# A 64-column product behind the first unit's products, and two planner costs, in an fp32 recurrence with a bilinear feed-forward block

## Chip, cores and metric

The kernel runs on one core of one Trainium2 chip. The metric is device microseconds of one launch. TensorE (PE, with its weight loads PEld), VectorE (DVE), ScalarE (ACT), GpSimd (POOL) and SyncE (SP, which issues most of the DMAs) each work through a queue of their own, in order.

## What is computed

A gated linear recurrence over 4 batches x 8 heads, 768 steps, head size 48, and behind it a bilinear feed-forward block on the 3072 rows of 384 channels that it gives:

```python
f = 1.0 / (1.0 + np.exp(-f_logit))
for t in range(S):
    state = f[:, :, t, :, None] * state + np.einsum('bhd,bhe->bhde', k[:, :, t], v[:, :, t])
    y[:, :, t] = np.einsum('bhd,bhde->bhe', q[:, :, t], state)
...
x = y.transpose(0, 2, 1, 3).reshape(B * S, H * D)
out = ((x @ w_a) * (x @ w_b)) @ w_out     # 384 -> 1536 -> 384
```

## The kernel before

**Attention.** The recurrence is cut into 16 units of four heads and half a sequence (384 steps), and a unit into six chunks of 64 steps. The front of a unit (`front_parts`) forms two sigmoids on ACT (L323, L326), an affine step on POOL (L329), running products by scans on DVE (L333, L346), and multiplies them into k and q (L350). Then follow on TensorE `scores` (L396), `turn` (L421, copied by `turned` on ACT, L428 and L430), `gains` (L445), `within` (L504) and `across` (L530), all with small tiles; on DVE `mask` (L409) and `carry` (L472, L474), which adds the chunks' gains up to states, six or five sums per unit. `across` adds what the states before a chunk give to the chunk. `out_of_bank` (L553) copies the result out of PSUM, and DMAs (L575) store it to `xT`, transposed as the feed-forward block wants it.

**Feed-forward.** Rows go through in eight blocks of 384. The first two blocks use `up` (L619): per 128 features six products of 384 columns, ACT's copy of one factor (L640) and DVE's product (L645), while the float64 weights are still being loaded and converted (`from_double`, L71 to L83). Later blocks use `up_triples` (L745): 15 block products v1 to v5, v6, u1 to u5, r2, r3, t1, t2 in place of 18, for each of four triples j. ACT copies results out of PSUM (L1333, the line where the planner calls a step), DVE adds them (L737). At the end of a triple, `finish` issues v6, its copy, and the product a * b over 1152 columns, also in L737. `finish` of triple j runs inside triple j+1. Copies of the next triple reuse buffers that the sums and the product read. `down` (L847) multiplies by `w_out` with seven products for eight, copied and added on ACT and DVE (L862 to L882).

**Order.** For the first 19 of the 24 feature groups of the two first blocks the order is written by hand. There `across(0)` of the first unit follows `gains(1)`, then come its copies and stores (`y_of(0)`), further carried sums of unit 1, `across(1)`, and two unread products of 384 columns (`keep_up`) that only keep TensorE going:

```python
across(0)
y_of(0)
end(1)
carried(1, range(1, NJ - 1))
first_scan, *scans = parts[2][1]
emit_all([first_scan])
across(1)
keep_up(2, ps_y[:, 0])
```

The rest is ordered by a list planner when the program is built. `main` is the list of feed-forward steps in fixed order, where every TensorE step counts as a beat of 653 ns. Attention steps lie in six lines (`core`, `fore`, `loads` and so on), each with an engine, an assumed cost in ns and an offset. Before each main step, `fill` takes steps from the lines that fit. A step for another engine fits only if `delays` says no: `delays` walks the next 80 main steps and asks whether main steps of this engine, each with a load and a due beat, would end after the start of the TensorE beat that they are due for. A due of 0 means that a step has no due beat. The assumed costs are 870 for a scan L333, 385 for a scan L346, 880 for a product L350 or a mask, 930 and 750 for the sigmoids, 400 for a copy in a triple, 180 for a `carry`, 1280 for a triple's product.

Of the kernel before, what the change touches and what calls it, by code (L numbers as in the profile page):

```python
# [18 lines left out]
ALU = mybir.AluOpType  # L19
# [3 lines left out]
BLK = 384  # L23
# [7 lines left out]
SUB = 64  # L31
# [122 lines left out]
def by_quotients(ctx, tc, q, k, f_logit, v, moe_w_a, moe_w_b, moe_w_out, out, ident, weights, bad, ps_f):  # L154
    nc = tc.nc
# [21 lines left out]
    def fixed(shape, name):  # L177
        return fixedp.tile(shape, FP32, tag=name, name=name)
# [3 lines left out]
    for i in range(NSET):  # L182
        t = {n: fixed([128, 2, BLK], f"{n}_in{i}") for n in "qkf"}
# [28 lines left out]
    def unit(u):  # L212
        b, r = divmod(u, NH * NQ)
        return (b, *divmod(r, NQ))
# [89 lines left out]
    PE, DVE, ACT, POOL, SP = range(5)  # L304
    live = {}
    firsts = groups[:, len(EARLY)].rearrange("p (u n s) -> p u n s", u=NQ, n=2)
    products_of_f = {u: firsts[:, u] if u in FIRST else sets[u % NSET]["f"] for u in range(NU)}
    xT = {}

    def halves(x):  # L310
        return x.rearrange("p n s -> p (n s)")
# [48 lines left out]
    ps_x, ps_y = (ps_a.tile([128, 2, 512], FP32, tag=n, name=n) for n in ("ps_x", "ps_y"))  # L360
    idle = list(range(4))

    def tokens(n, c, p):

        return slice(n * BLK + c * C + p * SUB, n * BLK + c * C + p * SUB + SUB)

    def each():
        for n in range(2):
            for c in range(NC):
                yield n, c, (n * NC + c) * SUB  # L370
# [142 lines left out]
    def across(u):  # L513

        b, half, qd = unit(u)
        qf, st, ps = halves(sets[u % NSET]["q"]), live[u]["st"], live[u]["y"]

        order = [(n, c, o, p) for n, c, o in each() for p in range(2)]
        if u in FIRST:

            order = sorted(order[::-1], key=lambda x: -x[3])
        elif half:
            order = [(n, c, o, p) for n, c, o in reversed(list(each())) for p in range(2)]
        for n, c, o, p in order:
            j = 2 * c + p
            if j == half == 0:
                continue
            for h in range(2):
                r, e = slice(R * h, R * h + D), R * (p ^ h)
                nc.tensor.matmul(  # L530
                    ps[p][e:e + D, o:o + SUB],
                    lhsT=st[j][r, n],
                    rhs=qf[r, tokens(n, c, p)],
                    start=False,
                    stop=True,
                    skip_group_check=True,
                )
# [49 lines left out]
    def products(blk):  # L587

        first = (NTG, 0)[blk] if blk < 2 else blk % 2
        return groups[:, first:first + NTG].rearrange("p g (k t) -> p g k t", k=NFT)  # L590
# [11 lines left out]
    def on(engine, load, due, do, *args, copied=False):  # L602
        return engine + COPIED * copied, load, beats[0] + due if due else 1 << 30, do, *args
# [46 lines left out]
    NI, NJ3 = 3, NFT // 3  # L650
# [88 lines left out]
    def up_triples(blk):  # L739

        to, tail = products(blk), None

        def emit(ps, name, j, start):
            for g in range(2):
                nc.tensor.matmul(  # L745
                    ps[:, g],
                    lhsT=sums_of_w[name][:, g, 128 * j:128 * j + 128],
                    rhs=sums_of_x[blk][name],
                    start=start and g == 0,
                    stop=True,  # L750
                    skip_group_check=True,
                )

        def times(ps, name, j, start=False):
            return on_pe(BEAT, emit, ps, name, j, start)

        def copy(due, x, ps):
            return on(ACT, 400, due, nc.scalar.copy, x, ps)

        def finish(j, c, out, v):  # L760
            yield times(v, "v6", j)
            yield copy(5, out[1, 0], v)
            a, b = (
                c[:, g].rearrange("p k i t -> p k (i t)").rearrange("p k (g t) -> p g k t", g=NTG) for g in range(2)
            )
            yield on(DVE, 1280, 0, add_steps, to.rearrange("p g (k j) t -> p j g k t", k=NI)[:, j], a, b, ALU.mult, copied=True)

        for j in range(NJ3):
            v, u, r, t = (ps_f[i][:, 0:BLK].rearrange("p (g t) -> p g t", g=2) for i in free)
            free[:] = [free[i] for i in ((2, 1, 3, 0) if j < NJ3 - 1 else (2, 3, 1, 0))]  # L770
            c = (sums, last[:, 0:2 * NI * BLK])[j % 2].rearrange("p (g k i t) -> p g k i t", g=2, k=NI, i=2)
            out = {(k, i): c[:, :, k, i] for k in range(NI) for i in range(2)}
            if j % 2:
                at = thirds.index(down_first[0])
                pairs = [thirds[(at + n) % 3] for n in (1, 2)]
            else:
                pairs = [last[:, PIECE * n:PIECE * n + PIECE] for n in range(2)]
            first, second = (x.rearrange("p (g n t) -> p g n t", g=2, n=2) for x in pairs)

            def add(due, k, i, ps, copied=False):  # L780
                return on(DVE, 550, due, add_steps, out[k, i], ps, out[k, i], copied=copied)

            yield times(v, "v1", j, True)
            yield copy(3, out[2, 0], v)
            if tail:
                yield from finish(*tail)
            yield times(u, "u1", j, True)
            yield copy(3, out[1, 1], u)
            yield times(r, "r2", j, True)
            yield add(6, 1, 1, r, True)  # L790
            yield times(v, "v2", j)
            yield copy(3, out[2, 1], v)
            yield times(u, "u2", j)
            yield copy(3, first[:, :, 1], u)
            yield times(t, "t1", j, True)
            yield copy(6, out[0, 0], t)
            yield times(v, "v3", j)
            yield copy(3, first[:, :, 0], v)
            yield on(DVE, 870, 0, add_steps, c[:, :, 1:3, 1], c[:, :, 1:3, 1], first, copied=True)
            yield times(u, "u3", j)  # L800
            yield copy(3, out[0, 1], u)
            yield times(r, "r3", j, True)
            yield add(6, 2, 1, r)
            yield times(v, "v4", j)
            yield copy(3, second[:, :, 1], v)
            yield times(u, "u4", j)
            yield add(3, 0, 0, u)
            yield times(t, "t2", j)
            yield add(5, 0, 1, t)
            yield times(v, "v5", j)  # L810
            yield copy(2 if j == NJ3 - 1 else 3, second[:, :, 0], v)
            yield times(u, "u5", j)
            yield add(3, 2, 0, u)
            yield on(DVE, 870, 0, add_steps, c[:, :, 0], c[:, :, 0], second, copied=True)
            tail = j, c, out, v
        yield from finish(*tail)

    down_first = [thirds[0]]

# [106 lines left out]
    def core_parts(s):  # L926


        u = s - 1
        if u < 2 * NQ:  # L930
            yield PE, 1000, 0, scores, s
        elif s < NU:
            yield PE, 1600, 0, within_and_scores, u
        else:
            yield PE, 1000, 20 * BEAT, within, u
        if s < NU:
            yield DVE, 880, 0, mask, s
            yield PE, 760, 0, turn, s
            yield ACT, 700, 0, turned, s
        if u < 2 * NQ:  # L940
            yield PE, 1000, 0, gains, s
        elif s < NU:
            yield PE, 1550, 0, gains_and_across, u
        else:
            yield PE, 1000, 0, across, u
        if s < NU:
            for j in range(NJ - 1 if unit(s)[1] == NH - 1 else NJ):
                yield DVE, 180, 0, carry, s, j
            if unit(s)[1] < NH - 1:
                yield DVE, 320, 0, hand_on, s  # L950
        if u >= 2 * NQ:
            for part in range(3):
                yield ACT, 490, 0, out_of_bank, u, part
            begin, *stores = stores_of(u)
            yield SP, 0, 0, begin
            for do in stores:
                yield SP, ISSUE, 5000, do
# [41 lines left out]
    with tc.manual_schedule():  # L999
# [12 lines left out]
            for _, _, do, *args in steps:  # L1012
                do(*args)

        def keep_up(n, to):

            x = products_of_f[0][:, 0]
            for _ in range(n):
                nc.tensor.matmul(to[:, 0:BLK], lhsT=ident, rhs=x, start=True, stop=True)

        def y_of(u):
            for part in range(4 if u == NQ - 1 else 3):
                out_of_bank(u, part)
            stored(u)
            if u == NQ - 1:
                give_back(live[u]["y"])
# [40 lines left out]
        within(1)  # L1067
        gains(1, range(NC - 1, NC))
        across(0)
        y_of(0)  # L1070
        end(1)
        carried(1, range(1, NJ - 1))
# [98 lines left out]
        for blk in range(NBLK):  # L1171
# [5 lines left out]
            b, odd = divmod(blk, 2)  # L1177
# [508 lines left out]
```

## Time and profile before

| | |
|---|---|
| Runs | 594.01, 592.02, 594.11 us; median 594.01 |
| Profiled execution | 591.24 us, its span 589.2 us |
| Busy PE, DVE, ACT, POOL | 567.3, 410.6, 258.1, 88.5 us |
| PE rows | L619: 288 rows of 384 columns, mean 490 ns; L745 and L847: rows of 192 columns, mean 326 to 331 ns |
| Prologue, 0 to 34 us | PE busy 18.5 us |
| 34 to 126 us; 126 to 186 us | PE busy 92.0; 59.9 us |
| 186 to 235; 235 to 300; 300 to 390 us | PE busy 47.9 of 49; 64.9 of 65; 89.9 of 90 us |
| 390 to 589 us | PE busy 194.3 of 199 us |

The page gives busy time, the chain that ended last, and groups of instructions by line. An fp32 product appears on PE as two rows, and as two weight loads on PEld. A row's length is modelled and overlaps the next row's; the distance of two starts tells the pace. In the timeline a line is a run of like rows: start, length, engine, line, tiles, count, and in brackets the idle time before it with what ended it. "issue" means that the engine waited for nothing that the profile shows.

### The profile page before, as it was taken

Reading aid. Unit: us, or ns where it says so; the run is one execution under the profiler, and the core shown is the slowest. Engines: PE = TensorE matmul, PEld = TensorE weight load, DVE = VectorE, ACT = ScalarE, POOL = GpSimd, SP = SyncE. Lnnn points to the kernel's source line nnn. Section 1 sums busy time; section 2 is a strip of 40 time slices with the busy share of each in tenths; the row PEclk is TensorE's granted clock in tenths of the full one; section 3 lists DMA queues with packets and bytes.
Section 4 is the critical chain, followed back from the end, with each engine's and each line's share of the span. In section 5 each row is a group of like instructions: output and inputs, shape, how many; then the busy total and the mean of one; then the engine's idle time right before and its main releaser. Section 6 shows DMA issues by size and latency. Waiting matters only on the chain.

```text
span 589.2 us, 13937 instructions
## 1 busy us (share of the span) xinstructions
PE 567.3 (96%) x5794; PEld 510.0 (87%) x5794; DVE 410.6 (70%) x782; ACT 258.1 (44%) x494; POOL 88.5 (15%) x73
## 2 busy tenths in 40 slices
PE   2889999999999999999999999999999999999996
PEld 1656655558999999999999999999999999999996
DVE  6898544699878768877896687928784256745741
ACT  5588768642133553247521355335431345144300
POOL 6465557462000000000000000000000000000000
PEclk9999999999999999999999999999999999999999
DMA  8699399099442403044004400040001100000001
GB/s 208 190 265 312 110 291 252 0 184 189 124 120 63 101 2 102 10 122 101 2 12 118 129 1 2 5 125 21 3 1 48 48 1 0 2 28 1 0 29 32
DMA packets 33576, 49.42 MB, mean 84 GB/s; under 512 B 3984, under 2 KB 25280, under 8 KB 33504
## 3 DMA queue, kind: packets, MB, share of 16 engines
q1 hardware_dynamic: 30000, 42.19, 25.9%
q0 software_dynamic: 3088, 5.92, 5.9%
q8 instruction: 47, 0.77, 0.6%
q10 hardware_dynamic: 416, 0.34, 0.2%
q14 instruction: 25, 0.20, 0.1%
HBM read 33.23 MB, written 4.72 MB: 64 GB/s over the span
## 4 chain that ended last, share of the span: by engine, by line
PE 90%; DVE 5%; issue 2%; DMA 1%; ACT 1%; SPq 0%; DVEq 0%; ACTq 0%
PE ps_f L745 37%; PE ps_f L847 28%; PE ps_f L619 16%; PE ps_y L504 2%; PE ps_x L396 2%; PE ps_x L445 1%; PE ps_y L530 1%; PE ps_x L421 1%; DVE sums L737 1%; DVE inv L346 1%; DVE groups L333 1%; DMA f_in<-in_f_logit_dram 1%; DVE q_in L350 1%; DMA xT<-groups 0%; DVE groups L737 0%
## 5 line engine op out<-in xcount | busy, mean ns | idle before, releaser
L619 PE MATMUL ps_f<-xT,w_ba 128*128 128x384 f32 x288 | 95.7, 490 | 2.8 <-DMA xT<-y 2.6
L619 PEld LDWEIGHTS ps_f<-xT,w_ba 128*128 128x128 f32 x288 | 53.7, 190 | 39.8 <-DVE start L341 3.2
L1333 ACT COPY sums<-ps_f 128x384 f32<-128x384 f32 x120 | 57.6, 481 | 69.6 <-PE ps_f L745 61.4
L1333 ACT COPY groups<-ps_f 128x384 f32<-128x384 f32 x120 | 57.8, 481 | 59.4 <-PE ps_f L745 39.0
L745 PE MATMUL ps_f<-xT,w_ba 128*128 128x192 f32 x384 | 78.5, 327 | 0.0
L745 PEld LDWEIGHTS ps_f<-xT,w_ba 128*128 128x128 f32 x384 | 64.8, 190 | 0.2
L73 POOL TENSOR_SCALAR sums<-sums 128x768 f32<-128x768 f32 (+1 forms) x20 | 51.2, 2561 | 33.6 <-ACT sums L71 33.5
L745 PE MATMUL ps_f<-groups,w_ba 128*128 128x192 f32 x288 | 55.1, 327 | 0.0
L745 PE MATMUL ps_f<-x_sums,raw 128*128 128x192 f32 x288 | 54.2, 331 | 0.7 <-DVE sums L737 0.6
L329 POOL TENSOR_SCALAR inv<-inv 128x768 f32<-128x768 f32 x14 | 12.7, 904 | 261.6 <-ACT inv L326 237.6
L847 PE MATMUL ps_f<-w_out,groups 128*128 128x192 f32 x288 | 51.8, 329 | 0.0
L847 PE MATMUL ps_f<-w_out,sums 128*128 128x192 f32 x288 | 51.4, 326 | 0.0
L745 PEld LDWEIGHTS ps_f<-x_sums,raw 128*128 128x128 f32 x288 | 46.9, 190 | 3.5 <-DVE sums L737 1.1
L847 PE MATMUL ps_f<-spare,sums 128*128 128x192 f32 x288 | 49.6, 327 | 0.0
L745 PEld LDWEIGHTS ps_f<-groups,w_ba 128*128 128x128 f32 x288 | 48.0, 190 | 0.2 <-ACT groups L1333 0.2
L847 PEld LDWEIGHTS ps_f<-w_out,groups 128*128 128x128 f32 x288 | 47.2, 190 | 0.7
L847 PEld LDWEIGHTS ps_f<-w_out,sums 128*128 128x128 f32 x288 | 47.4, 190 | 0.1
L847 PEld LDWEIGHTS ps_f<-spare,sums 128*128 128x128 f32 x288 | 47.0, 190 | 0.2
L737 DVE TENSOR_TENSOR sums<-ps_f,sums 128x384 f32<-128x384 f32 x60 | 32.8, 553 | 15.5 <-PE ps_f L745 14.2
L737 DVE TENSOR_TENSOR sums<-sums,groups 128x768 f32<-128x768 f32 x36 | 34.7, 963 | 12.4 <-ACT groups L1333 12.0
L745 PE MATMUL ps_f<-xT,raw 128*128 128x192 f32 x192 | 39.6, 329 | 0.5 <-ACT sums L1333 0.5
L745 PE MATMUL ps_f<-x_sums,w_ba 128*128 128x192 f32 x192 | 39.3, 327 | 0.1
(150 smaller groups left out, 848.0 us busy)
## 6 DMA issues: line engine op xcount, KB each, us to landing
raw<-w_ba POOLq DMA_DIRECT2D x11, 512.0 KB, 8.3
k_in<-in_k_dram SPq DMA_DIRECT2D x32, 144.0 KB, 4.3
q_in<-in_q_dram SPq DMA_DIRECT2D x32, 144.0 KB, 4.4
v_in<-in_v_dram SPq DMA_DIRECT2D x16, 288.0 KB, 5.1
raw<-in_moe_w_out_dram SPq DMA_DIRECT2D x6, 768.0 KB, 4.9
out_dram<-o SPq DMA_DIRECT2D x22, 192.0 KB, 1.9
f_in<-in_f_logit_dram SPq DMA_DIRECT2D x28, 144.0 KB, 3.0
xT<-y SPq DMA_DIRECT2D x44, 72.0 KB, 2.1
```

The lines of the kernel that those rows point to most:

```text
L73: nc.gpsimd.tensor_scalar(h, h, HI_MIN, HI_MAX, ALU.max, ALU.min)
L329: nc.gpsimd.tensor_scalar(inv, inv, EXP_K, 1.0, ALU.mult, ALU.add)
L333: nc.vector.tensor_tensor_scan(F[:, c], F[:, c], none, math.exp(MIDDLE), ALU.mult, ALU.add)
L346: nc.vector.tensor_tensor_scan(inv[:, w], inv[:, w], none[:, 0:C], first, ALU.mult, ALU.add)
L350: nc.vector.tensor_tensor(halves(t[nm]), halves(t[nm]), by, ALU.mult)
L396: nc.tensor.matmul(ps[h][SUB * p:SUB * p + SUB, o:o + SUB], lhsT=kf[r, tokens(n, c, p)], rhs=qf[r, tokens(n, c, p)], start=True, stop=True,)
L504: nc.tensor.matmul(ps[p][e:e + D, o:o + SUB], lhsT=t["v"][r, n, c, h * D:h * D + D], rhs=at[r, h, o:o + SUB], start=o == 0, stop=True, ski ...
L619: nc.tensor.matmul(ps[nm][:, 0:BLK], lhsT=w[:, kt, ft * 128:ft * 128 + 128], rhs=xT[blk][:, kt], start=kt == 0, stop=kt == NKT - 1,)
L737: nc.vector.tensor_tensor(to, x, y, op)
L745: nc.tensor.matmul(ps[:, g], lhsT=sums_of_w[name][:, g, 128 * j:128 * j + 128], rhs=sums_of_x[blk][name], start=start and g == 0, stop=Tru ...
L847: nc.tensor.matmul(to, lhsT=x[:, i // 2, i % 2], rhs=w[:, NI * (i % 2) + i // 2], start=start and i == 0, stop=i == HFT - 1, skip_group_ch ...
L1333: do(*args)
```

## The change

Three edits. First, `keep_up` gets a width, and one unread product of 64 columns into the first bank of `ps_y` is put on TensorE directly behind `across(0)`. Second, the planner's cost of a `carry` goes from 180 to 290. Third, the product in `finish` gets a due time: 5 beats after the beat of v6, where it had none; the last triple of a block keeps none.

```diff
-        def finish(j, c, out, v):
+        def finish(j, c, out, v, due=5):
             yield times(v, "v6", j)
             yield copy(5, out[1, 0], v)
...
-            yield on(DVE, 1280, 0, add_steps, to.rearrange("p g (k j) t -> p j g k t", k=NI)[:, j], a, b, ALU.mult, copied=True)
+            yield on(DVE, 1280, due, add_steps, to.rearrange("p g (k j) t -> p j g k t", k=NI)[:, j], a, b, ALU.mult, copied=True)
...
-        yield from finish(*tail)
+        yield from finish(*tail, 0)
...
             for j in range(NJ - 1 if unit(s)[1] == NH - 1 else NJ):
-                yield DVE, 180, 0, carry, s, j
+                yield DVE, 290, 0, carry, s, j
...
-        def keep_up(n, to):
+        def keep_up(n, to, width=BLK):
...
-            x = products_of_f[0][:, 0]
+            x = products_of_f[0][:, 0, 0:width]
             for _ in range(n):
-                nc.tensor.matmul(to[:, 0:BLK], lhsT=ident, rhs=x, start=True, stop=True)
+                nc.tensor.matmul(to[:, 0:width], lhsT=ident, rhs=x, start=True, stop=True)
...
         across(0)
+        keep_up(1, ps_y[:, 0], SUB)
         y_of(0)
```

No other instruction is added or taken away. The second and third edit change only what the planner assumes, and so where the attention steps stand between the feed-forward steps.

## The prediction

> **What bounds the kernel now.** I read the page first, then the waits of TensorE, then the timeline at each place where TensorE stood still. The page's first lines:
>
> ```profile
> span 589.2 us, 13937 instructions
> PE 567.3 (96%) x5794; PEld 510.0 (87%) x5794; DVE 410.6 (70%) x782; ACT 258.1 (44%) x494; POOL 88.5 (15%) x73
> ```
>
> TensorE (PE) is busy 96%, and the product rows L619, L745 and L847 make most of the chain that ended last. The change takes no product away, so it can only win idle time: 589.2 - 567.3 = 21.9 us. Of that, 10.4 us is the wait for the first products, some 5 us the tail after the last product, and 2.6 us the wait for the first rows of xT. What the change aims at lies in two places.
>
> The first is the prologue. The timeline of PE, 22 to 28 us (start, length, line, xcount; the bracket is idle time and what ended it), and one line of ACT:
>
> ```profile
> 22.82 0.56 PE L445 MATMUL ps_f<-v_in,kT 64*48 64x48 f32 x28 [0.47 <-issue]
> 23.35 0.89 PE L504 MATMUL ps_f<-at,v_in 64*48 64x64 f32 x48
> 24.06 0.36 PE L445 MATMUL ps_f<-v_in,kT 64*48 64x48 f32 x16
> 24.25 1.01 PE L530 MATMUL ps_x<-q_in,st 48*48 48x64 f32 x36
> 26.54 0.26 PE L530 MATMUL ps_x<-q_in,st 48*48 48x64 f32 x2 [1.29 <-issue]
> ...
> 26.90 1.45 ACT L553 COPY y<-ps_x 48x384 f32<-48x384 f32 x3 [2.76 <-PE ps_x L530]
> ```
>
> The last two of `across(0)`'s 20 products (four of its 40 rows) come 1.29 us after the others, and ACT's copies of the first unit, which feed the stores to xT, wait for them. It looks as if they were stuck in the array until `across(1)` came. But count: between the two "issue" gaps stand 28 + 48 + 16 + 36 = 128 product rows, and PEld's rows of the same stretch are 27 + 48 + 16 + 37 = 128 weight loads, together exactly 256. The queue list has one 16 KB instruction packet of q8 in the 3 us before 26.54, and `across(1)`'s sums had ended at 26.09, so the wait for them was over by then. I read the gap as TensorE waiting for its next block of instructions.
>
> The second place is the list scheduler's part, from 126 us on. Stalls there, from the timeline:
>
> ```profile
> 214.03 0.94 ACT L326 ACTIVATE inv<-f_in,less 128x768 f32<-128x768 f32 x1
> 215.32 0.49 ACT L1333 COPY sums<-ps_f 128x384 f32<-128x384 f32 x1
> 215.86 0.92 PE L745 MATMUL ps_f<-xT,raw 128*128 128x192 f32 x4 [0.48 <-ACT sums L1333]
> ...
> 221.10 0.95 DVE L333 TENSOR_TENSOR_SCAN f_in<-f_in,zero 128x384 f32<-128x384 f32 x1
> 221.97 1.00 DVE L737 TENSOR_TENSOR sums<-ps_f,sums 128x384 f32<-128x384 f32 x2
> 222.56 1.73 PE L745 MATMUL ps_f<-x_sums,raw 128*128 128x192 f32 x9 [0.58 <-DVE sums L737]
> ...
> 284.26 0.96 DVE L350 TENSOR_TENSOR k_in<-k_in,inv 128x768 f32<-128x768 f32 x1
> 285.14 0.55 DVE L737 TENSOR_TENSOR sums<-ps_f,sums 128x384 f32<-128x384 f32 x1
> 285.74 0.92 PE L745 MATMUL ps_f<-x_sums,w_ba 128*128 128x192 f32 x4
> ...
> 341.41 0.94 ACT L326 ACTIVATE inv<-f_in,less 128x768 f32<-128x768 f32 x1
> 342.34 0.47 ACT L1333 COPY groups<-ps_f 128x384 f32<-128x384 f32 x1
> ```
>
> Each time a filler of attention work (sigmoid L326, scan L333, product L350) stands on ACT or DVE ahead of a copy or sum that TensorE needs. Undisturbed L745 rows start 0.163 us apart. Against that spacing the starts lose 0.74 us at 215 (0.64 and 0.10 on the row after it), 0.84 at 222, 0.35 at 285 with 0.2 behind it, 0.40 at 342. The whole is 2.5 us, 0.4% of the time. Some 0.2 us at the end of each block's triples comes from the last v6 waiting for v5's copy and stays.
>
> **The Trainium skill.** "Runtime: NRT & Kernel Launch", section Instruction fetch mechanics: instructions are refilled in 16 KiB blocks of 256, and crossing a block is mostly hidden. The trace agrees with the 256 to the row, and here the crossing is not hidden. "TensorE: Matmul & The Clock Gate", Part 3, The mechanism: matmuls are "strict FIFO, no reordering"; nothing there says that one needs a successor to finish, and no row here shows it. "VectorE: DVE Perf Modes", section on the TRN2 errata, prices an fp32 add at (N+151)/0.96 ns, 257 for the 96 elements of a carried sum; the trace has 252.
>
> **The change part by part.**
>
> *The unread product.* It adds one product of `ident` with 64 columns into `ps_y`: two weight loads and two product rows, after `across(0)`. Nothing before it moves, so the same instructions of `across(0)` lie behind the block boundary and still come at 26.54; ACT's copies still start at 26.90. Gain 0. The cost falls on `across(1)`, which is queued behind it. For the switch from small tiles to the full array I take the row after `across(1)`: 0.15 us to the first `keep_up` start and 0.43 to the next, of which 0.34 are its 384 columns, so 0.43 - 0.34 + 0.06 = 0.15 for 64. The way back to small tiles costs 0.09 elsewhere, plus 0.06 for the second pass. Sum 0.45, less what the array overlaps: 0.35. Who waits: DVE's two copies of the second unit (now 27.78), then DVE's queue: scans of unit 2, the last rows of `w_a`, its k and q, then pieces 2 and 3 of the weights, almost without a gap until 40 us. ACT's copies (28.37) and SP's stores (28.37, 30.50) have their own queues ahead of them and do not move, so the first `up` stays at 31.81. But a weight load at 39.62 waits 0.38 us for DVE's `w_ba` already, and there the delay reaches TensorE; nothing behind it has room to take it back. I take +0.3. Bounds: 0 (DVE's small gaps absorb it) to +0.45. If the product does push the last products out, the copies start 1.3 us sooner, but `w_a`'s first row (30.95) and k, q (36.08, scores now at 36.80) hold TensorE back: -0.6 at best.
>
> *Carried sum 290 instead of 180, and a due time of 5 beats for a triple's product.* No instruction is added or removed; the planner only puts fillers elsewhere. In the built order, DVE, ACT and PE are rearranged; the blocks of attention products on TensorE move by 0 to 4 beats (0.65 us each) and stay as many, so their switching cost is unchanged. POOL's and SP's instructions are the same, some a few places later. At the four stalls:
>
> - 215: two carried sums instead of three stand ahead of u5's sum (-0.27), and L326 now follows the copies of v6 and u1 instead of standing between v1's and v6's. u1's copy ends near 214.8, before u2 at 215.2, so the stall goes. Next late is u2's copy, behind L326 and L323 (0.94 + 0.19 + 0.86): about 217.6 against u3 at 217.2, with switching 0.55 lost again.
> - 222: a scan moves from ahead of `first`'s sum to between the sums of r3 and u4. u4's sum ends near 221.5, when u5 needs it: -0.84. With the line above: -1.58 + 0.55, -1.0.
> - 285: L350 leaves the place ahead of u5's sum, which then ends near 285.3 instead of 285.69; the five carried sums ahead of a product in the block go behind it: -0.5.
> - 342: L326 goes behind v5's copy: -0.4.
>
> Sum -1.9. Against it stand new places. In the second block of triples the mask L409, which waits for scores, now stands ahead of u5's sum of the first triple. Scores and within take 1.6 us, mask 0.96, sum 0.55: 3.1 us after u5, when u1 is due at 3.15 to 3.2. With v1's copy and a product behind that, 0.1 to 0.3; for two or three such places +0.4. Bounds for the planner's part: -2.5 (all stalls gone, none new) to +1.5 (as many new as it had, none gone). I take -1.9 + 0.4 = -1.5.
>
> Together +0.3 - 1.5 = -1.2 us. The profiled execution took 591.24 us (span 589.2 and 2.0 around it), which gives 590.0. The median of the three runs is 594.01, 2.8 above that execution; on the median's scale, 594.01 - 1.2 = 592.8.
>
> **Rivals.**
>
> *The product pushes.* The last products of `across(0)` do come when something follows. For it: they come together with `across(1)`. Against: 256 exactly, and the sums were ready 0.45 us earlier. Time: 594.01 - 0.6 - 1.5 = 591.9; with all stalls gone too, 594.01 - 0.6 - 2.5 = 590.9.
>
> *Nothing to see.* The new order trades stall for stall: 594.01 + 0.3 = 594.3.
>
> *Slower: scores run ahead of q.* The planner's costs for a unit's front on DVE (2 scans at 870, 6 at 385, two products at 880, 80 and 90) sum to 5.98 us; the trace's rows (0.943, four of 0.474 and two of 0.424, 0.955, 0.16, 0.17) give 6.9, so it believes q ready 0.9 us early. Due times squeeze fillers into fewer gaps. If q's product slips past the start of `scores`, TensorE waits on `q_in` L350, as it does once, 0.28 us at 126. The slack is 1.1 to 2.1 us in the units I looked at (q ends 204.48, scores 205.62), so it decides once a unit loses more than 1.1. Six units at 0.6 us: +3.6 + 0.3, 597.9.
>
> **How the numbers follow.** About 0.5% (3.0 us) is what a measurement of this kernel can tell from no change; the three runs alone spread by 2.1. Forecast 0.50, product pushes 0.20, nothing to see 0.18, scores ahead of q 0.12. The forecast and the push stay within 3 us by their centres, but with their best ends (-2.5 and -3.1) and a median's scatter of about 1 us, a quarter to a third of each pair passes it: faster 0.25. Slower is the last rival and little else: 0.11. The rest, 0.64, is within. Range: down to the push with all stalls gone and half a microsecond of scatter, 590.0; up to nothing gained and 1.5 us of new stalls, 595.8.
>
> **What would show it.** Right: L530's last `ps_x` rows still at 26.54 behind an "issue" gap of 1.29, L553 still at 26.90; the new product between them and `across(1)`; `across(1)` 0.3 to 0.4 later; the stalls at 215, 222, 285 and 342 gone or smaller; PE's waits on L1333 and L737 shorter. Wrong: L553 near 25.6 (the push); new idle time of PE on L350 or L409; a first L619 that moves from 31.81; a time under 590 or over 596.

## The result, and the profile after

| | median | runs | beside it, before | ratio, 95% interval |
|---|---|---|---|---|
| changed kernel | 590.07 us (587.99 to 592.57) | 10 | 593.38 us (10 runs) | 0.9946 [0.9928, 0.9964] |
| the same again, later | 590.62 us (589.29 to 592.41) | 22 | 592.39 us (59 runs) | 0.9981 [0.9970, 0.9993] |

The change makes the kernel faster: by 3.3 us in the first comparison, by 1.8 us in the second. The two intervals do not overlap (0.9964 and 0.9970 are their near ends), so the size of the gain is known to a few tenths of a per cent only. The forecast was 592.8 us, a gain of 1.2 us on a scale of 594.01; 590.07 us lies just inside the lower end of its range, 590.0 us.

The profiled execution took 590.78 us (before: 591.24 us). The head of the page:

```profile
span 588.9 us, 13930 instructions
PE 568.4 (97%) x5796; PEld 510.7 (87%) x5796; DVE 412.0 (70%) x782; ACT 257.5 (44%) x494; POOL 90.4 (15%) x73
```

PE has the two product rows more that were added (5796 for 5794). Its span is 0.3 us shorter. That small sum hides larger terms, found by comparing the starts of the same products in both traces. The prologue, up to the scores L396 of unit 2, is longer by 2.5 us (39.31 for 36.80 us). The middle, from the last L619 to the last product, is shorter by 1.4 us (446.52 for 447.93 us). The tail behind the last product is shorter by 1.6 us (3.69 for 5.25 us, from the start of that product). With 0.2 us more between the scores and the last L619 the sum is 2.5 + 0.2 - 1.4 - 1.6 = -0.3 us. Only the gain in the middle comes back in every profiled launch with the new order.

**The prologue.** The timeline of the changed kernel, PE and one row of ACT (start, length, engine, line, tiles, count; in brackets idle time and what ended it):

```profile
22.69 0.56 PE L445 MATMUL ps_f<-v_in,kT 64*48 64x48 f32 x28 [0.35 <-issue]
23.34 0.89 PE L504 MATMUL ps_f<-at,v_in 64*48 64x64 f32 x48
24.05 0.36 PE L445 MATMUL ps_f<-v_in,kT 64*48 64x48 f32 x16
24.23 1.01 PE L530 MATMUL ps_x<-q_in,st 48*48 48x64 f32 x36
...
27.52 0.32 PE L530 MATMUL ps_x<-q_in,st 48*48 48x64 f32 x4 [2.27 <-issue]
27.76 0.43 PE L1020 MATMUL ps_y<-groups,ident 128*128 128x64 f32 x2
27.87 1.45 ACT L553 COPY y<-ps_x 48x384 f32<-48x384 f32 x3 [4.10 <-PE ps_x L530]
28.13 1.90 PE L530 MATMUL ps_f<-q_in,st 48*48 48x64 f32 x40
...
29.95 2.40 PE L1020 MATMUL ps_y<-groups,ident 128*128 128x384 f32 x4
```

Between the two "issue" gaps stand again 28 + 48 + 16 + 36 = 128 product rows. The last four rows of `across(0)` still come behind the gap, and ACT's copies still wait for them. The new product (L1020 with 64 columns) stands between them and `across(1)`, 0.37 us from its start to the start of `across(1)`. What is new is the pace behind it: 40 rows in 1.90 us, for 1.15 us in other launches. The table by stage says why (PE, PEld, DVE, ACT, POOL busy; then the granted clock):

```profile
25.50:29.00 3.50, 1.48 (x26) 1.34 (x29) 1.11 (x2) 1.11 (x3) 0.21 (x1) 0.90 0.05 15
29.00:32.50 3.50, 3.50 (x33) 2.21 (x30) 2.31 (x5) 1.57 (x4) 1.97 (x4) 0.62 0.36 102
```

In this launch TensorE ran at half clock from 28.28 us on, for 3.41 us. Before, the profiled launch had none in the prologue; its half clock lies behind the last product (583.94 us), where it costs nothing, and makes up all of its mean clock of 0.998:

```profile
586.41:589.18 2.77, 0.00 (x0) 0.00 (x0) 0.00 (x0) 0.00 (x0) 0.00 (x0) 0.50 0.02 2
```

The half-clock stretch of the changed kernel's launch follows the long gap; it is not something that every launch of the changed kernel has.

**The middle.** PE, ACT and DVE at the places of the four old stalls and at three new ones, from the timeline of the changed kernel (it runs 2.8 us later than the one before at 216 us, and 1.4 us later at 297):

```profile
216.09 0.81 PE L745 MATMUL ps_f<-x_sums,w_ba 128*128 128x192 f32 x4
216.19 0.48 ACT L1335 COPY sums<-ps_f 128x384 f32<-128x384 f32 x1 [2.87 <-DVE groups L737]
216.56 0.48 ACT L1335 COPY groups<-ps_f 128x384 f32<-128x384 f32 x1
216.74 1.46 PE L745 MATMUL ps_f<-groups,w_ba 128*128 128x192 f32 x8
216.94 0.49 ACT L1335 COPY sums<-ps_f 128x384 f32<-128x384 f32 x1
...
217.31 0.95 ACT L326 ACTIVATE inv<-f_in,less 128x768 f32<-128x768 f32 x1
218.04 0.81 PE L745 MATMUL ps_f<-xT,raw 128*128 128x192 f32 x4
...
263.59 0.96 DVE L409 TENSOR_TENSOR at<-ps_x,causal 128x768 f32<-128x768 f32 x1 [2.10 <-PE ps_x L396]
...
264.46 0.55 DVE L737 TENSOR_TENSOR sums<-ps_f,sums 128x384 f32<-128x384 f32 x1
...
265.06 0.92 PE L745 MATMUL ps_f<-x_sums,w_ba 128*128 128x192 f32 x4
...
295.38 0.94 DVE L409 TENSOR_TENSOR at<-ps_x,causal 128x768 f32<-128x768 f32 x1
...
296.24 0.94 DVE L333 TENSOR_TENSOR_SCAN f_in<-f_in,zero 128x384 f32<-128x384 f32 x1
...
297.11 0.99 DVE L737 TENSOR_TENSOR groups<-ps_f,groups 128x384 f32<-128x384 f32 x2
...
297.69 1.59 PE L745 MATMUL ps_f<-x_sums,raw 128*128 128x192 f32 x8 [0.52 <-DVE groups L737]
...
345.76 0.86 ACT L323 ACTIVATE f_in<-f_in 128x768 f32<-128x768 f32 x1
...
346.50 0.87 ACT L1335 COPY groups<-ps_f 128x384 f32<-128x384 f32 x2
...
347.04 0.92 PE L745 MATMUL ps_f<-xT,raw 128*128 128x192 f32 x4 [0.18 <-ACT groups L1335]
```

The first seven rows are the place of the old stall at 215: the sigmoid L326 now follows the three copies, and PE's starts go on at 0.163 us a row. By the same measure of starts the stalls of 0.64, 0.74, 0.24 and 0.30 us at 215, 222, 285 and 342 are gone. In their place stand three new ones: 0.18 at 264.7 and 0.74 at 297, each behind a mask L409 (the second behind a scan L333 as well), and 0.34 at 346.5 behind a sigmoid L323.

### The profile page after: what moved, and what is told of

Its sections match the earlier page's. It is cut to its first block, busy times and chain, and to the rows that moved or that the text cites. A ratio compares the mean times of both kernels' runs of the same rounds, so it can differ in the third digit from the quotient of the medians.

```text
span 588.9 us, 13930 instructions
## 1 busy us (share of the span) xinstructions
PE 568.4 (97%) x5796; PEld 510.7 (87%) x5796; DVE 412.0 (70%) x782; ACT 257.5 (44%) x494; POOL 90.4 (15%) x73
## 4 chain that ended last, share of the span: by engine, by line
PE 91%; DVE 5%; issue 2%; ACT 1%; DMA 1%; SPq 0%; DVEq 0%; ACTq 0%
PE ps_f L745 39%; PE ps_f L847 28%; PE ps_f L619 15%; PE ps_y L504 2%; PE ps_y L530 2%; PE ps_x L445 1%; PE ps_x L396 1%; PE ps_x L421 1%; DVE inv L346 1%; DVE q_in L350 1%; DVE groups L333 1%; DMA f_in<-in_f_logit_dram 1%; DVE at L409 0%; DVE groups L737 0%; DVE spare L346 0%
## 5 line engine op out<-in xcount | busy, mean ns | idle before, releaser
L619 PE MATMUL ps_f<-xT,w_ba 128*128 128x384 f32 x288 | 95.8, 490 | 0.7 <-DVE w_ba L83 0.6
L619 PEld LDWEIGHTS ps_f<-xT,w_ba 128*128 128x128 f32 x288 | 53.7, 190 | 37.8 <-ACT spare L75 1.2
L73 POOL TENSOR_SCALAR sums<-sums 128x768 f32<-128x768 f32 (+1 forms) x20 | 52.6, 2629 | 34.5 <-ACT sums L71 34.4
```

Of the source, the lines that this page charges most:

```text
L73: nc.gpsimd.tensor_scalar(h, h, HI_MIN, HI_MAX, ALU.max, ALU.min)
L619: nc.tensor.matmul(ps[nm][:, 0:BLK], lhsT=w[:, kt, ft * 128:ft * 128 + 128], rhs=xT[blk][:, kt], start=kt == 0, stop=kt == NKT - 1,)
```

## The experiments

Four theories were to be told apart. **Order**: the planner's new order takes away stalls in the middle, and that is the gain. **Block**: the last rows of `across(0)` wait for TensorE's next instructions, not for a successor that pushes them. **Push**: the unread product pushes them out. **Clock**: unread products matter through the granted clock behind them. The runs e5 to e11 were made once e1 to e4 had shown what was left over.

All results beside each other. Medians and ratios are those of the comparison; the means of time and granted clock are over the same runs. Runs of one session shared the runs of the kernel before.

| run | median us | runs | ratio to before | mean us | mean clock |
|---|---|---|---|---|---|
| before, session 1 | 593.11 | 51 | | 592.93 | 0.9958 |
| e1, product alone | 592.28 | 14 | 0.9989 [0.9971, 1.0008] | 592.31 | 0.9985 |
| e2, both planner edits | 591.24 | 14 | 0.9976 [0.9958, 0.9995] | 591.76 | 0.9959 |
| e3, due time alone | 592.59 | 14 | 0.9995 [0.9977, 1.0014] | 592.58 | 0.9961 |
| e4, carry cost alone | 591.58 | 22 | 0.9983 [0.9968, 0.9999] | 591.64 | 0.9962 |
| before, session 2 | 592.39 | 59 | | 592.32 | 0.9962 |
| e5, changed kernel again | 590.62 | 22 | 0.9981 [0.9970, 0.9993] | 590.88 | 0.9974 |
| e6, planner, longer `keep_up` | 590.19 | 22 | 0.9966 [0.9952, 0.9980] | 590.36 | 0.9981 |
| e7, e6 with the block shifted | 590.46 | 22 | 0.9968 [0.9955, 0.9981] | 590.50 | 0.9964 |
| before, session 3 | 593.23 | 39 | | 593.24 | 0.9951 |
| e8, longer `keep_up` alone | 592.05 | 22 | 0.9976 [0.9963, 0.9988] | 592.08 | 0.9975 |
| e9, no `keep_up` there | 593.05 | 14 | 1.0001 [0.9987, 1.0015] | 593.13 | 0.9927 |
| e10, e7 with still longer `keep_up` | 591.06 | 10 | 0.9960 [0.9944, 0.9976] | 591.01 | 0.9967 |
| e11, changed kernel, longer `keep_up` | 589.99 | 6 | 0.9949 [0.9932, 0.9966] | 590.13 | 0.9982 |

### The parts, one at a time

**The unread product alone.**

```diff
         across(0)
+        keep_up(1, ps_y[:, 0], SUB)
         y_of(0)
```

> The kernel before with the unread 64-column product alone; the planner as it was. Block theory (the gap in across of the first unit is TensorE waiting for its next 256 instructions): the last four of its 40 rows still come after the gap, ACT's first copy with them, across of the second unit 0.3 to 0.6 us later; time +0.1 to +0.6 us against the kernel before (ratio 1.000 to 1.001). Push theory (the product drives the last products out): no late rows, ACT's copies 1.3 us or more sooner; time -0.6 to -2.0 us (ratio 0.997 to 0.999).

Measured: 592.28 us, ratio 0.9989 [0.9971, 1.0008]. The middle is 447.93 us, as before. The timeline of PE:

```profile
26.29 0.32 PE L530 MATMUL ps_x<-q_in,st 48*48 48x64 f32 x4 [1.08 <-issue]
26.53 0.43 PE L1019 MATMUL ps_y<-groups,ident 128*128 128x64 f32 x2
26.90 1.15 PE L530 MATMUL ps_f<-q_in,st 48*48 48x64 f32 x40
27.98 1.56 PE L1019 MATMUL ps_y<-groups,ident 128*128 128x384 f32 x4
...
35.84 0.79 PE L421 MATMUL ps_y<-ident,k_in 112*128 112x112 f32 x6 [0.33 <-DVE k_in L350]
```

The gap and the four late rows are still there. The product pushes nothing out. From the end of the gap to `keep_up` behind `across(1)` it is 27.98 (the start of `keep_up`, in the fence) - 26.29 = 1.69 us, where before it was 27.64 - 26.54 = 1.10: the product holds `across(1)` up by 0.59 us (0.47 us against e3, whose launch took 1.22 us with the same order as before). PE now waits 0.33 us for the k of unit 2, DVE's chain being later. The first `up` L619 comes sooner: 31.08 - 26.29 = 4.79 us behind the gap's end, where before it was 31.81 - 26.54 = 5.27 us. So it is in all four profiled launches with the product (4.77 to 4.79 us, for 5.27 to 5.31 in before, e2, e3 and e4). The stores to `xT` in this stretch land sooner after their issue (medians of 2.3 to 2.5 us, without it 2.7 to 2.8); why is open. The time is not longer, and the mean clock is higher, 0.9985 for 0.9958. That was not expected.

**Both planner edits**, no product behind `across(0)`.

```diff
-        def finish(j, c, out, v):
+        def finish(j, c, out, v, due=5):
...
-                yield DVE, 180, 0, carry, s, j
+                yield DVE, 290, 0, carry, s, j
```

> The changed kernel without the unread product: carried sum 290 and due time 5 kept. If the planner carries the whole change, -3 to -4 us (ratio 0.993 to 0.995) with the product costing 0.3; if the middle of the trace says it all (TensorE 1.4 us sooner between 130 us and its last product), -1.0 to -2.0 us (0.9966 to 0.9983) and the rest of the 3.3 us is the product's.

Measured: 591.24 us, ratio 0.9976 [0.9958, 0.9995]. The middle is 446.71 us, 1.2 us less than before, as the second of the two expectations said. The same three new stalls are there.

**The due time alone.**

```diff
-        def finish(j, c, out, v):
+        def finish(j, c, out, v, due=5):
...
-            yield on(DVE, 1280, 0, add_steps, ..., copied=True)
+            yield on(DVE, 1280, due, add_steps, ..., copied=True)
...
-        yield from finish(*tail)
+        yield from finish(*tail, 0)
```

> The due time alone, carried sum back at 180, no unread product. Theory: the due time is what keeps scans and the five carried sums from standing ahead of a product, so it takes the stalls at 222 and 285: 1.0 of the 1.5 us of the planner's part. Rival: it does little alone, since the planner still counts 110 ns too few for each carried sum, and is within 0.5 us of the kernel before.

**The carry cost alone.**

```diff
-                yield DVE, 180, 0, carry, s, j
+                yield DVE, 290, 0, carry, s, j
```

> The carried sum at 290 alone, no due time, no unread product. Theory: it takes one carried sum and the sigmoid from ahead of the copies at 215, 0.3 to 0.6 us, and leaves 222 and 285. Rival: the two planner edits are one, and most of the gain comes already from the right cost, 1 us or more.

Measured: 592.59 and 591.58 us. The built programs tell more than the times here. With the due time alone the order of instructions is that of the kernel before on every engine. With the carry cost alone it is that of both edits together, where instructions stand at other places than before on TensorE, DVE, ACT and SP. So the due time does nothing in this kernel: the theories of e3 and e4 fall, and e4's rival holds. e3 is a second measurement of before, and e2 and e4 are two measurements of one program. Their 36 runs have a mean of (14 x 591.76 + 22 x 591.64) / 36 = 591.69 us, 1.24 us under the mean of the kernel before in their session.

**The changed kernel again.** No edit.

> The changed kernel as it is, timed beside the next two. Clock theory (the unread product does not push anything; it puts TensorE's work later into its idle stretch and so spares, in most runs, a stretch of 3.4 us at half clock): mean granted clock near 0.9985, time 0.5 to 1.0 us under the kernel with the planner's part alone, which was 1.2 to 1.4 under the kernel before; so -1.8 to -2.4 us (ratio 0.996 to 0.997). Rival: the -3.2 us of its first timing is real, and the product and the new order help each other: ratio 0.9946 again.

Measured: 590.62 us, ratio 0.9981 [0.9970, 0.9993]; in means 1.44 us under before. The middle is 446.69 us. Of the first comparison's 3.3 us about half came back, so the rival (0.9946 again) falls; the clock, 0.9974, stayed short of the 0.9985 that the clock theory named.

### The block and the clock

**A longer `keep_up` in place of the product.** The planner's edits, no product behind `across(0)`, four unread products of 384 columns behind `across(1)` where there were two.

```diff
-        keep_up(1, ps_y[:, 0], SUB)
...
         across(1)
-        keep_up(2, ps_y[:, 0])
+        keep_up(4, ps_y[:, 0])
```

> The planner's part, no product behind across of the first unit, and four unread products of 384 columns in place of two behind across of the second unit, where TensorE waits for xT anyway. Clock theory: mean clock 0.999 or more, nothing on the path of across, so 0.3 to 0.9 us faster than the changed kernel. Rival (the place behind the first unit's across matters, not the clock): as the planner's part alone, ratio 0.9975 to 0.9985, and clock 0.996.

Measured: 590.19 us, 0.4 us under e5 by medians and 0.5 by means, with overlapping intervals; clock 0.9981.

**The block shifted.** As e6, and two unread products fewer ahead of the place, which moves all that follows by eight instructions (four weight loads, four product rows).

```diff
         gains(0)
-        keep_up(4, ps_f[idle[-1]])
+        keep_up(2, ps_f[idle[-1]])
```

> The kernel with four unread products at the end, and with two instead of four in the first keep_up after gains of unit 0: eight TensorE instructions fewer ahead of the first unit's across. Block theory: the gap falls eight instructions later, so all 40 rows of across of the first unit come before it, four rows of the second unit's across before it too; ACT's first copy starts 1.0 to 1.5 us before the gap's end instead of 0.35 after it; first L619 0.3 to 1.0 us sooner, time 0.3 to 0.8 us under the kernel with four. Rival (the rows stick to the wait for the carried sums): again the last four rows of the first across come with the second's, and no gain.

Measured: 590.46 us, no gain over e6. But the block theory is shown by it. The timeline, PE and ACT:

```profile
24.46 1.11 PE L530 MATMUL ps_x<-q_in,st 48*48 48x64 f32 x40
...
27.30 1.15 PE L530 MATMUL ps_f<-q_in,st 48*48 48x64 f32 x40 [1.73 <-DVE f_in L333]
```

```profile
25.65 1.45 ACT L553 COPY y<-ps_x 48x384 f32<-48x384 f32 x3 [1.73 <-PE ps_x L530]
```

All 40 rows of `across(0)` now come in one piece, with nothing behind them for 1.7 us, and ACT's copies follow at once. In the eight other profiles up to here 36 rows came ahead of the gap and four behind it. A shift by eight instructions, four product rows and four weight loads, moves just the four late rows ahead of the gap (none of `across(1)` came with them, though four of its rows were expected to); a successor is not needed. (The bracket names the scan L333, the last signal seen; the gap stands behind the same count of instructions as before.) The DMA records support this. In all 13 traces one 16 KB packet of q8, a queue of kind "instruction", lands ahead of the gap's end, and the gap ends 1.27 to 1.49 us later. It lands at 25.27 us before (gap's end 26.54), at 26.10 in the changed kernel (27.52), at 25.82 in e7 (27.30), at 26.74 in e8 (28.22) and at 27.65 in e10 (28.93). So the length of the gap follows the packet, whose start alone varies from 23.4 to 26.6 us. What it wins is lost again: `across(1)` still comes at 27.30 us, and then PE waits for DVE, 0.58 us at 36.25 for k (L350) and 0.74 us at 38.79 for `w_ba` (L83).

**The longer `keep_up` alone.** The kernel before, with four in place of two behind `across(1)`.

```diff
         across(1)
-        keep_up(2, ps_y[:, 0])
+        keep_up(4, ps_y[:, 0])
```

> The kernel before with four unread products of 384 columns behind across(1) in place of two (keep_up(2) -> keep_up(4)); nothing else changed, neither the planner nor a product behind across(0). Clock theory: TensorE is busy for longer in the stretch behind across(1), so a launch falls to half clock less often; the mean granted clock of its runs rises from about 0.996 (before) to about 0.998, and the time falls by 0.6 to 1.0 us against the kernel before. The middle, from the last L619 to the last product, stays at 447.9. Rival 1 (the gain of the run with the planner's costs and long unread products, 0.7 us more than the planner's costs alone, was scatter): no gain, clock as before. Rival 2 (they stand in the way of the first up): +0.4 to +1 us, since two more products are 4 rows of about 0.35 us at full clock, and twice that at half clock.

Measured: 592.05 us, ratio 0.9976 [0.9963, 0.9988], 1.2 us less in means; clock 0.9975 for 0.9951. The middle is 447.99 us, as before. This gain lies outside the planner's part, and of the rivals scatter falls, and standing in the way falls for the mean. In its profiled launch, the slowest of its runs (594.19 us), the unread products do stand in the way: the packet came late, half clock lasted 6.83 us, and the first `up` started at 35.13 us straight behind them, 6.91 us after the gap's end.

**None at all** behind `across(1)`, otherwise the kernel before.

```diff
         across(1)
-        keep_up(2, ps_y[:, 0])
+        keep_up(0, ps_y[:, 0])
```

> The kernel before without the two unread products behind across(1) (keep_up(2) -> keep_up(0)); nothing else changed. It is the kernel before with less of the supposed cause. Clock theory: TensorE stands idle behind across(1) until the first up, so more launches fall to half clock there: mean granted clock of the runs below the 0.996 of before, about 0.994, half clock at 28 to 33 us or later in most launches, time +0.6 to +1.5 us. Rival (the clock is set elsewhere, and time and clock merely vary together): clock and time as before, within 0.5 us.

Measured: clock 0.9927, as expected; time 593.05 us, ratio 1.0001 [0.9987, 1.0015], against the expected 0.6 to 1.5 us more. The profiled launch (595.38 us, the slowest of its runs) had half clock for 10.2 us from 28.88 on. The table by stage, columns as above:

```profile
29.00:32.50 3.50, 0.00 (x0) 0.00 (x0) 3.40 (x11) 2.64 (x5) 2.71 (x4) 0.50 0.50 137
32.50:36.00 3.50, 2.73 (x5) 1.55 (x6) 3.47 (x7) 2.35 (x4) 2.97 (x1) 0.50 0.72 170
36.00:40.00 4.00, 4.00 (x9) 2.17 (x8) 3.73 (x9) 1.97 (x4) 1.61 (x2) 0.61 1.03 373
```

Up to the first `up` at 33.27 us, 4.4 of the 10.2 us, TensorE has nothing to do (0.00 us busy in the first row), and half clock costs nothing; the rest falls on the `up`. So the clock's mean is no price by itself. What counts is which rows run inside such a stretch, and taking the two products out may also have cleared the way. The runs do not part these two.

**Shifted, and longer still.** As e7, with six unread products behind `across(1)`.

```diff
         across(1)
-        keep_up(4, ps_y[:, 0])
+        keep_up(6, ps_y[:, 0])
```

> The run with the block shifted (carry cost 290, due time, first keep_up 2 in place of 4 products, no product behind across(0)), with six unread products behind across(1) in place of four. There all 40 rows of across(0) lie ahead of the block boundary and ACT's first copy came 1.6 us sooner, and the time was no better than without the shift; its mean clock was lower (0.9964 against 0.9981). Theory A (the lower clock hid the shift's gain): clock back to 0.998 or more, time 0.5 to 1 us under that of the long products without the shift, near 589.6. Theory B (DVE's chain of unit 2, k and q L350 and the weights L83, takes over as the bound at 36 to 39 us whatever the stores do): within 0.4 us of 590.4 whatever the clock; PE waits on L350 and L83 stay.

Measured: 591.06 us, ratio 0.9960 [0.9944, 0.9976] beside e7's 0.9968. The clock, 0.9967, did not come back to 0.998, so theory A was not put to its test; the time is 0.6 us above theory B's 590.4, in a session whose runs of before were 0.8 us slower by medians. Inconclusive. There is no sign that the shift is worth anything.

**The changed kernel with the longer `keep_up`.** 

```diff
         keep_up(1, ps_y[:, 0], SUB)
...
         across(1)
-        keep_up(2, ps_y[:, 0])
+        keep_up(4, ps_y[:, 0])
```

> The changed kernel with four unread products behind across(1) in place of two: it differs from the run with the planner's costs and long unread products (590.4 mean, 590.2 median) by the one product of 64 columns behind across(0) alone. With the clock already kept by the long products, the small product can no longer help by the clock. Theory (product costs its place on the path, +0.3 as worked out before; its gain is the clock): 0.2 to 0.7 us slower than that run, 590.7 to 591.0. Rival (the product helps otherwise, by the order of instructions): equal to or faster than 590.4, and below the changed kernel.

Measured: 589.99 us in six runs, ratio 0.9949 [0.9932, 0.9966]. By its median it is the fastest kernel here, but the interval overlaps those of the changed kernel and of e6. The 0.2 to 0.7 us that the product was to cost over e6 are not seen in the times: 590.13 for 590.36 in means, and 3.1 us under before for 2.0, each in its own session.

### What the traces say of the product's price and the clock's

The stretch from the end of the gap to unit 2's first scores L396, by starts in each profiled launch (aligned on the first product, so a few hundredths off the timelines):

| | half clock in the prologue | gap ends | scores | stretch |
|---|---|---|---|---|
| before; e3 (same order) | none | 26.54; 26.01 | 36.80; 36.19 | 10.26; 10.18 |
| e1; e5; e11 (with the product) | none | 26.29; 26.77; 26.07 | 36.71; 37.25; 36.54 | 10.42; 10.48; 10.47 |
| e2; e4 (no product) | 3.41 us from 32.5; 32.95 | 26.23; 26.77 | 37.85; 38.38 | 11.62; 11.61 |
| changed kernel | 3.41 us from 28.28 | 27.53 | 39.32 | 11.79 |
| e6 (longer `keep_up`) | 3.41 us from 28.5 | 26.74 | 36.79 | 10.05 |
| e8 (longer `keep_up` alone) | 6.83 us from 27.88 | 28.11 | 39.56 | 11.45 |
| e9 (no `keep_up`) | 10.24 us from 28.88 | 27.05 | 40.79 | 13.74 |
| e10 (shifted, still longer) | 3.41 us from 29.80 | 28.96 | 40.19 | 11.23 |

At full clock the three launches with the product need 10.46 us and the two without 10.22, so the product costs 0.24 us of path. A half-clock stretch costs 1.3 to 1.4 us more, if it falls on `across(1)` or the first `up`. In e6 it fell on unread products, and cost nothing. That is no rule: in e8 and e10 it fell mostly on unread products too, and there these held up the first `up`, to 6.91 and 6.69 us after the gap's end. The timeline of e2 shows the usual case:

```profile
27.28 1.56 PE L1020 MATMUL ps_y<-groups,ident 128*128 128x384 f32 x4
31.50 5.80 PE L619 MATMUL ps_f<-xT,w_ba 128*128 128x384 f32 x12 [2.66 <-DMA xT<-y]
```

and the table by stage of e2, then of e1, for the stretch in which TensorE waits for the first rows of `xT`:

```profile
29.00:32.50 3.50, 1.00 (x3) 0.68 (x4) 3.43 (x11) 2.69 (x3) 2.71 (x5) 0.99 0.61 168
32.50:36.00 3.50, 3.50 (x7) 1.72 (x6) 3.46 (x6) 2.39 (x5) 2.35 (x2) 0.52 0.85 222
```

```profile
29.00:32.50 3.50, 1.95 (x6) 0.59 (x4) 3.40 (x11) 2.36 (x4) 2.21 (x5) 1.00 0.57 168
32.50:36.00 3.50, 3.16 (x11) 1.60 (x11) 3.46 (x7) 2.85 (x5) 2.59 (x2) 1.00 0.92 257
```

In e2 PE was busy for 1.00 of 3.50 us, and the 12 rows of the first `up` took 5.80 us at a clock of 0.52 for 4.43 us in e1. In e1, where `across(1)` and `keep_up` come later behind the product and the first `up` sooner, PE was busy for 1.95 us and the clock stayed. The Trainium skill, "TensorE: Matmul & The Clock Gate", Part 1, What's actually happening, says that a monitor halves TensorE's clock after an idle window of about 3.4 us and that the windows run freely. The traces agree in the length: the stretches are 3.41, 6.83 and 10.24 us, and the full-clock stretches between them are multiples of 3.41 us too. So each launch has windows of its own, whose edges can be counted in steps of 3.41 us from the start of any half-clock stretch, the one in the tail too. In before and in e2 the window with TensorE's wait for `xT` is:

```profile
30.05:33.46 3.41, 1.53 (x4) 0.69 (x5) 3.34 (x12) 3.26 (x4) 2.60 (x3) 1.00 0.67 179
29.05:32.46 3.41, 0.96 (x3) 0.68 (x4) 3.34 (x11) 2.65 (x3) 2.62 (x4) 1.00 0.63 172
```

Before went on at full clock, e2 fell to half. In six of the seven launches with a half-clock stretch PE was busy for 0.80 to 1.16 us in the window ahead of it, and in no window of the prologue behind which the clock stayed full for less than 1.53 us. The exception is e6, which fell after a window with 1.92 us. So a window need not be wholly idle, and PE's busy time does not decide alone. With the product, TensorE's wait for the first `up` is 1.5 us long in e1 and e5, without it 2.5 to 2.7 us in before, e2, e3 and e4: `keep_up` comes later and `up` sooner, which leaves less idle time for a window to catch.

## Why the prediction was right, and where it was not

**The planner's part: right in its sum, with some luck.** Forecast -1.5 us; the middle gives -1.2 to -1.7 in the six profiled launches with the carry cost 290 and no shifted block (446.27 to 446.71 us for 447.93), and 36 runs give -1.24. The four stalls went, as forecast. Its terms were off in both directions. The follow-on at u2's copy (0.55 us) did not come. The order is the one forecast: both sigmoids stand ahead of that copy (L326 at 217.31 us, L323 at 218.62). But the copy started at 219.36 us and took 0.47, so it ended 0.16 us ahead of u3's first row at 219.99; the prediction had it 0.4 us too late for u3. The new places cost more than the 0.4 us allowed: 0.74 + 0.34 + 0.18 = 1.26 us. Of these the 0.18 us is the one named, a mask ahead of u5's sum, at its forecast size of 0.1 to 0.3; the other two were covered only by the allowance. Several small stalls of before between 230 and 372 us, together 0.5 us, went unforeseen. That the misses nearly cancel is luck. With the shifted block the middle is 446.86 (e7) and 446.28 us (e10).

**The due time: a step that failed unseen.** The prediction took "carried sum 290 and a due time of 5 beats" as one and credited them together. The built order shows that the second changes nothing. The sum did not suffer, but the reason given was half empty.

**The block: right.** The count of 256, the gap and the four rows behind it came back in the changed kernel, the shift by eight instructions moved all four rows ahead of the gap, and the gap ends with the instruction packet in every trace. Push falls with it: ACT's copies started at 27.87 us, not near 25.6. They did not start at 26.90 either, as the prediction named for its proof, since the gap was 2.27 us long in this launch in place of 1.29.

**The product's price: right as a cost, wrong as a net.** `across(1)` was to be held up by 0.35 us and is held up by 0.59, so that term was too small; of it +0.3 us was to reach the path, and the traces give +0.24 at full clock, so about half of the delay is taken up before unit 2's scores. The step that failed on the path is "the first `up` stays": counted from the gap's end it comes 0.5 us sooner with the product, which the prediction's list of signs had under wrong. And the launches with it are no slower. The term left out is the granted clock. In e1 the mean clock rose by 0.0027, which over 590 us is 1.6 us of lost clock, or 1.6 / 1.71 = 0.9 half-clock stretches of 3.41 us fewer per launch (if the whole difference lies in the prologue; the mean also counts half clock in the tail, which took from 0 to 2.8 us in the 13 profiled launches). At 1.3 to 1.4 us each this would be -1.2 us, with the product's cost -1.0; the runs show -0.6, with an interval from -1.7 to +0.5. In e5 against e2 and e4, over two sessions, the net is about -0.2 us, less than the intervals can show. The prediction read the profiled launch of before, whose clock was full up to the last product, and took it for the usual one; of the 51 runs of before in session 1, 42 have a mean clock of 0.997 or less.

That the clock is the cause is supported and not settled. For it: e8 raises the clock and shortens the time with the middle unchanged (e1 does too, but the interval of its time includes no change), and launches with a half-clock stretch on path products reach the scores later. Against it: e9 lowers the clock by 0.0024 and loses nothing. And within one kernel time and clock go together (before in session 1: 591.03 us in the 5 runs at 0.9985 or more, 593.14 us in the other 46), which a late instruction packet would also bring about (e8's launch: gap, delay and half clock at once), and a long tail as well, since it adds time and half clock behind the last product.

**The slower rival** (scores ahead of q) did not show in the middle. PE's waits on L350 appear at 18.94, 37.81 and 39.31 us only, in the prologue; the last two come where DVE's chain is late after the long gap.

**The size.** From 593.38 to 590.07 us is 3.3 us: 1.2 us the order, perhaps some tenths the product. The rest, 1.5 to 2 us, did not come back when the kernel was run again beside more runs of before; between these two comparisons the median of before moved by 1.0 us and that of the changed kernel by 0.55. What differs between the sessions stays open; sessions 1, 2 and 3 ran on three different chips, and for the first comparison the chip is not on record. The statement that about 0.5% is what can be told apart was wide for one comparison, whose intervals are 0.12 to 0.19% to each side, but the two comparisons of the same two kernels differ by 0.35%.

## What to carry to other kernels

Build each planner edit alone and compare the orders before crediting it: an edit that moves no instruction needs no theory. When TensorE's rows stop with "issue" as the reason, count instructions between such gaps, and look for the instruction packet ahead of their end, before looking for data or a successor. And before pricing unread products on TensorE, look at the granted clock over all runs, not in the one profiled launch: their place decides whether they cost path or save a half-clock stretch.

## What the runs showed of the hardware

- TensorE's half-clock stretches come in multiples of 3.41 us. One of them cost 1.3 to 1.4 us where products of the path ran in it (e2, e4, the changed kernel) and nothing on unread products in e6; in e8 and e10 half clock on unread products held up the products behind them. Six of seven launches fell to half clock after a window of 3.41 us with 0.80 to 1.16 us of busy PE, one after 1.92 us.
- A block of 256 instructions of small tiles is used up in about 2.4 us (22.82 to 25.2 us before), while the next ones come about 4 us apart (23.30 and 27.30 us in e7). The gap at the end of such a block varied from 1.0 us (e3) to 3.1 us (e8) by starts, with the same instructions ahead of it; it ended 1.27 to 1.49 us after a 16 KB instruction packet had landed, in all 13 traces.
- The tail behind the last product took 3.63 to 5.63 us, from the last product's start, over the profiled launches, though nothing in it was changed.
